# The low halves of the first MoE's third weight matrix: from one VectorE operation to two on Pool

## Chip, cores and metric

The kernel runs on one core of a Trainium2 chip. The metric is the device time of one execution in microseconds (us). Engines are named as the profile names them: PE is TensorE's matmul, PEld its weight load, DVE is VectorE, ACT is ScalarE, POOL is GpSimd, SP is SyncE, which issues the DMAs.

## What is computed

Causal attention with a forgetting bias over 4 batches, 8 heads, 576 positions and 64 columns per head; its output, seen as 2304 tokens of 512 columns, goes through two feed-forward blocks ("MoE" in the code), one after the other:

```python
rms = np.sqrt(np.mean(x * x, axis=-1, keepdims=True) + 1e-06)
xn = x / rms * rms_g
g = xn @ w_gate                       # 512 -> 1536
silu = g * (1.0 / (1.0 + np.exp(-g)))
val = xn @ w_val                      # 512 -> 1536
x = silu * val @ w_out                # 1536 -> 512: the matrix of this change
h = x @ w_in                          # second block, 512 -> 2048
return (h - np.tanh(h)) @ w_out2
```

The weights arrive as 64-bit floats, and the kernel decodes them itself.

## The kernel before

Every large product is made of three fp16 matmuls: each operand is split into a high half (the value rounded to fp16) and a low half (the rest). `mm3` issues high times high (line 693), high times the other's low half (694) and low times high (695).

The tokens are cut into six blocks of 384. `moe1_groups(j)` lists the work of block j: 24 up-projections, in turn `up1_g` (gate) and `up1_v` (value), of 12 matmuls each, and then four down-projections `down1` of 36 matmuls each. Between these groups the main loop steps the attention forward by a unit (a few heads of one query tile), so that the tokens of the next block are ready in time. A unit is: scores on PE (lines 452, 453), exponential on ACT (460), the causal mask on POOL (462), high half on ACT (467), low half on POOL (474), then products with v on PE (496 to 498). Its row maxima come earlier, from PE (409) and DVE (411).

Products of a group land in one of two PSUM buffers `mm`. The buffer of a gate group is read by ACT (710, tanh) and then DVE (711), that of a value group by DVE (720); ACT then makes the high half `sh` (721) and POOL the low half `sl` (722). The buffer of a down-projection is read by ACT (731). PE may write a buffer again only after its last reader.

The third matrix `w_out` is the tile `wo`, twelve pieces of 128 x 512, three for each of the four down-projections. While block 0 runs, each piece is loaded, decoded on DVE (559 to 561), squared on ACT (250); a sum over a group of three gives its scale `tau` (chain of small DVE operations, lines 666 to 669, and `iom` on POOL, 670); then `conv` splits the piece by `split`: ACT writes the high half (575), DVE the low half (576). Where these lie matters:

```python
    def slot_f(W, n):                       # the piece in fp32
        return W[:, n + 1, :].bitcast(FP32)
    def slot_h(W, n):
        return W[:, n, 0:512]
    def slot_l(W, n):
        return W[:, n, 512:1024]
```

The fp32 piece n - 1 fills exactly the place in which the two halves of piece n go. So the high half of piece n can be written only when the low half of piece n - 1 has been made: ACT, the engine of the low half, ACT, and so on, in series through all twelve pieces. Below, "slot n" is piece n counted from 0; slots 0 to 2 belong to the first down-projection.

The order of instructions on each engine is not written out by hand. A scheduler takes the program in the order of the code and sets the order by its own estimates of the costs; every engine then works through its queue strictly in that order. Loads of the next batch (q as `stv`, k as `stk`) run through SP's queue; ACT squares them on landing (line 250).

Of the kernel before, what the change touches and what calls it, by code (L numbers as in the profile page):

```python
# [11 lines left out]
ACTF = mybir.ActivationFunctionType  # L12
ALU = mybir.AluOpType
# [27 lines left out]
def tile_forget_attention_moe_moe2(ctx, tc, qa, qb, kt, va, vb, va0, vb0, s, wg, wv, wo, rg, win, wo2, out):  # L41
# [28 lines left out]
    V, A, G, P, SY = nc.vector, nc.scalar, nc.gpsimd, nc.tensor, nc.sync  # L70
# [17 lines left out]
    WO = w1.tile([128, 13, 1024], FP16, name="wo")  # L88
# [11 lines left out]
    def sm_tile(dtype=FP32):  # L100

        p, tag = (ps_mm, "mm") if early[0] else (ps_sm, "sm")
        return p.tile([128, 512], dtype, name=tag, tag=tag)
# [21 lines left out]
    def small(p, shape, dtype=FP32, tag=None):  # L125
        cnt[0] += 1
        return p.tile(shape, dtype, name=tag or f"sc{cnt[0]}", tag=tag or f"sc{cnt[0]}")

    def pow2inv(p, src, shape, emin, tag):
        e = small(p, shape, I32, tag + "e")  # L130
        V.tensor_scalar(out=e, in0=src.bitcast(I32), scalar1=24, scalar2=None, op0=ALU.logical_shift_right)
        V.tensor_scalar(out=e, in0=e, scalar1=float(emin), scalar2=50.0, op0=ALU.max, op1=ALU.add)
        V.tensor_scalar(out=e, in0=e, scalar1=23, scalar2=None, op0=ALU.logical_shift_left)
        sg = small(p, shape, FP32, tag + "s")
        V.reciprocal(out=sg, in_=e.bitcast(FP32))
        return e.bitcast(FP32), sg

    def ones_sum(psum, ss, n):
        P.matmul(out=psum[:, 0:n], lhsT=ones_f, rhs=ss, start=True, stop=True)
# [109 lines left out]
    def sq_accum(src, acc, junk=None):  # L249
        A.activation(out=src if junk is None else junk, in_=src, func=ACTF.Square, accum_out=acc)  # L250
# [300 lines left out]
    def decode(dst, src, raw):  # L551

        if src.dtype != I32:
            SY.dma_start(out=dst, in_=src)
            return
        with hold(1):
            SY.dma_start(out=raw, in_=src)
        d, hi, lo = dst.bitcast(I32), raw[:, :, 1], raw[:, :, 0]
        V.tensor_scalar(out=d, in0=hi, scalar1=3, scalar2=0x3FFFFFFF, op0=ALU.logical_shift_left, op1=ALU.bitwise_and)
        V.scalar_tensor_tensor(out=d, in0=hi, scalar=-0x40000000, in1=d, op0=ALU.bitwise_and, op1=ALU.bitwise_or)  # L560
        V.scalar_tensor_tensor(out=d, in0=lo, scalar=29, in1=d, op0=ALU.logical_shift_right, op1=ALU.bitwise_or)

    def slot_f(W, n):
# [9 lines that stand above are left out]
    def split(W, n, sc):  # L573
        src, hi, lo = slot_f(W, n), slot_h(W, n), slot_l(W, n)
        A.activation(out=hi, in_=src, func=ACTF.Copy, scale=sc)
        V.scalar_tensor_tensor(out=lo, in0=src, scalar=sc, in1=hi, op0=ALU.mult, op1=ALU.subtract)  # L576

    def raw_tile(p, bufs):
        return p.tile([128, 512, 2], I32, name="raw", tag="raw", bufs=bufs)

    def raw_slots(W, n):

        return W[:, n:n + 2, :].bitcast(I32).rearrange("p a (c w) -> p (a c) w", w=2)

    def junk16(raw):
        return raw[:, 0:128, :].bitcast(BF16).rearrange("p a b -> p (a b)")
# [50 lines left out]
    def wo_tasks(p):  # L637
        tasks = []
        tl = {}

        def first():
            sm3 = small(const, [128, 3], FP32, "sm3")
            for j in range(3):
                V.tensor_copy(sm3[:, j:j + 1], sig_s[j])
            smin = small(const, [128, 1], FP32, "smin")
            V.tensor_reduce(out=smin, in_=sm3, op=ALU.min, axis=AX.X)
            wos["ismin"] = small(const, [128, 1], FP32, "ismin")
            V.reciprocal(out=wos["ismin"], in_=smin)
            wos["rho"] = small(const, [128, 3], FP32, "rho")
            V.reciprocal(out=wos["rho"], in_=sm3)  # L650
            V.tensor_scalar(out=wos["rho"], in0=wos["rho"], scalar1=smin, scalar2=None, op0=ALU.mult)
            wos["iom"] = small(const, [128, 4], FP32, "iom")

        def piece(g, k):
            n = 3 * g + k
            raw = raw_slots(WO, 9 + 2 * (n // 2 % 2)) if n < 8 and n % 2 else raw_tile(p, 2)
            decode(slot_f(WO, n), wo[g, :, k], raw)
            if k == 0:
                wos["ss", g] = small(const, [128, 3], FP32, f"woss{g}")
            sq_accum(slot_f(WO, 3 * g + k), wos["ss", g][:, k:k + 1], junk16(raw))  # L660

        def chain(g):
            ps = sm_tile()
            ones_sum(ps, wos["ss", g], 3)
            nm = small(const, [128, 1], FP32, f"won{g}")
            V.tensor_reduce(out=nm, in_=ps[:, 0:3], op=ALU.add, axis=AX.X)
            isg, sg = pow2inv(const, nm, [128, 1], 37, f"wo{g}")
            tl["tau", g] = small(const, [128, 3], FP32, f"tau{g}")
            V.tensor_scalar(out=tl["tau", g], in0=wos["rho"], scalar1=sg, scalar2=None, op0=ALU.mult)
            G.tensor_scalar(out=wos["iom"][:, g:g + 1], in0=isg, scalar1=wos["ismin"], scalar2=1.0, op0=ALU.mult, op1=ALU.mult)  # L670

        def conv(g, k):
            split(WO, 3 * g + k, tl["tau", g][:, k:k + 1])

        tasks.append(first)
        for g in range(4):
            for k in range(3):
                tasks.append(lambda g=g, k=k: piece(g, k))
            tasks.append(lambda g=g: chain(g))
            for k in range(3):  # L680
                tasks.append(lambda g=g, k=k: conv(g, k))
        return tasks
# [243 lines left out]
    def need(T):  # L926
        return sum(len(units(x)) for x in range(T + 1)) + 2
# [26 lines left out]
    while last0 not in done_norm:  # L954
# [3 lines left out]
        n = min(left[0], 1)  # L958
# [5 lines left out]
    for j in range(NBLK - 1):  # L964
        last = BLOCK_TILES[j + 1][1] - 1
        s0 = steps[0]
        n = min(need(last), total) - s0
# [435 lines left out]
```

## Time and profile before

| | us |
|---|---|
| three runs, median (lowest to highest) | 1070.36 (1068.99 to 1070.47) |
| the profiled execution | 1068.06 |
| its span in the trace | 1066.3 |
| PE busy in the span | 973.4 (91%) |
| DVE busy | 679.9 (64%) |
| ACT busy | 606.6 (57%) |
| POOL busy | 320.6 (30%) |

The span is the time between the first and the last instruction; 1.8 us of the execution lie around it. A matmul of 384 columns shows about 0.33 us but follows its predecessor after 0.16 us, since matmuls are pipelined. What PE costs is therefore read from the distance of starts, and what it loses from its idle time, with the engine that ended it.

### The profile page before, as it was taken

Reading aid. Unit: us, or ns where it says so; the run is one execution under the profiler, and the core shown is the slowest. Engines: PE = TensorE matmul, PEld = TensorE weight load, DVE = VectorE, ACT = ScalarE, POOL = GpSimd, SP = SyncE. Lnnn points to the kernel's source line nnn. Section 1 sums busy time; section 2 is a strip of 40 time slices with the busy share of each in tenths; the row PEclk is TensorE's granted clock in tenths of the full one; section 3 lists DMA queues with packets and bytes.
Section 4 is the critical chain, followed back from the end, with each engine's and each line's share of the span. In section 5 each row is a group of like instructions: output and inputs, shape, how many; then the busy total and the mean of one; then the engine's idle time right before and its main releaser. Section 6 shows DMA issues by size and latency. Waiting matters only on the chain.

```text
span 1066.3 us, 19297 instructions
## 1 busy us (share of the span) xinstructions
PE 973.4 (91%) x7472; PEld 616.0 (58%) x7472; DVE 679.9 (64%) x1472; ACT 606.6 (57%) x1172; POOL 320.6 (30%) x405
## 2 busy tenths in 40 slices
PE   1488878799899999999999899999999999999998
PEld 1366545456566666666666555655666666666664
DVE  8987998975585641574553878579792683438500
ACT  6589657766675763676767456446571462225400
POOL 5121266323462542364456102100200251015200
PEclk9977988999999999999999999999999999999999
DMA  8614524231212112210200970142102000000000
GB/s 266 260 36 105 179 88 134 73 100 61 65 38 53 23 46 70 82 28 17 58 19 11 292 247 5 45 135 68 60 1 82 8 2 16 23 23 1 8 23 30
DMA packets 49438, 76.81 MB, mean 72 GB/s; under 512 B 25890, under 2 KB 35202, under 8 KB 48834
## 3 DMA queue, kind: packets, MB, share of 16 engines
q1 hardware_dynamic: 49346, 75.58, 23.0%
q8 instruction: 58, 0.95, 0.4%
q14 instruction: 34, 0.28, 0.1%
HBM read 59.42 MB, written 9.55 MB: 65 GB/s over the span
## 4 chain that ended last, share of the span: by engine, by line
PE 62%; DVE 18%; DMA 8%; ACT 5%; issue 4%; POOL 1%; SPq 1%; ACTq 0%; DVEq 0%; POOLq 0%
PE m L693 10%; PE m L695 10%; PE m L694 10%; PE mm L693 8%; PE mm L695 8%; PE mm L694 8%; DMA stv<-qb 1%; DVE w L560 1%; PE st L452 1%; PE st L453 1%; DMA raw<-wo 1%; DVE tm L711 1%; DMA w<-wo 1%; PE pv L494 1%; DVE r L417 1%
## 5 line engine op out<-in xcount | busy, mean ns | idle before, releaser
L693 PE MATMUL mm<-xth,w 128*128 128x384 f16 x480 | 161.3, 336 | 24.3 <-DVE tm L711 18.2
L694 PE MATMUL mm<-xtl,w 128*128 128x384 f16 x480 | 161.0, 336 | 0.9 <-DMA xtl<-xl 0.9
L695 PE MATMUL mm<-xth,w 128*128 128x384 f16 x480 | 160.4, 335 | 0.1
L694 PEld LDWEIGHTS <-w 128*128 128x128 f16 x960 | 94.8, 99 | 86.1 <-issue 32.4
L695 PEld LDWEIGHTS <-w 128*128 128x128 f16 x960 | 94.7, 99 | 64.8 <-issue 5.0
L693 PEld LDWEIGHTS <-w 128*128 128x128 f16 x960 | 95.3, 99 | 62.2 <-issue 4.0
L693 PE MATMUL m<-dh,w 128*128 128x384 f16 x384 | 124.1, 326 | 0.7 <-ACT t L1269 0.7
L694 PE MATMUL m<-dl,w 128*128 128x384 f16 x384 | 124.4, 326 | 0.0
L695 PE MATMUL m<-dh,w 128*128 128x384 f16 x384 | 124.1, 326 | 0.0
L722 POOL TENSOR_TENSOR sl<-tm,sh 128x384 f16<-128x384 f32 x72 | 76.2, 1059 | 112.9 <-ACT sh L721 103.7
L474 POOL TENSOR_TENSOR phl<-pf,phl 128x512 f16<-128x512 f32 (+2 forms) x90 | 97.4, 1090 | 40.6 <-ACT phl L467 39.1
L462 POOL TENSOR_SCALAR_AFFINE_SELECT pf<-pf 128x128 f32<-128x128 f32 (+3 forms) x105 | 43.1, 413 | 175.9 <-ACT pf L460 172.4
L1261 POOL TENSOR_SCALAR io<-iso,isd 128x1 f32<-128x1 f32 x24 | 12.0, 501 | 257.1 <-ACT t L1269 257.1
L460 ACT ACTIVATE pf<-st,lnp,ilam 128x512 f32<-128x512 f32 (+2 forms) x105 | 73.0, 703 | 24.7 <-PE st L453 19.3
L1269 ACT ACTIVATE t<-m,io 128x384 f32<-128x384 f32 x24 | 13.8, 578 | 126.7 <-PE m L695 123.0
L693 PE MATMUL mm<-sh,wo 128*128 128x384 f16 x240 | 78.0, 326 | 2.3 <-DVE tm L711 2.3
L695 PE MATMUL mm<-sh,wo 128*128 128x384 f16 x240 | 78.2, 326 | 0.7 <-DVE wo L576 0.7
L694 PE MATMUL mm<-sl,wo 128*128 128x384 f16 x240 | 78.1, 326 | 0.0
L452 PE MATMUL st<-q,kl 128*128 128x128 f16 (+1 forms) x456 | 62.5, 216 | 9.1 <-DVE q L368 2.7
L1300 DVE SCALAR_TENSOR_TENSOR c<-m,sigma,c 128x768 f32<-128x768 f32 x32 | 32.5, 1015 | 57.3 <-PE m L695 55.6
L1289 POOL TENSOR_TENSOR dl<-c,dh 128x768 f16<-128x768 f32 x28 | 48.0, 1730 | 54.9 <-ACT dh L1288 54.9
L711 DVE SCALAR_TENSOR_TENSOR tm<-tm,mm 128x384 f32<-128x384 f32 x60 | 32.9, 548 | 43.9 <-ACT tm L710 41.4
(369 smaller groups left out, 2571.0 us busy)
## 6 DMA issues: line engine op xcount, KB each, us to landing
raw<-wo SPq DMA_DIRECT2D x16, 512.0 KB
w<-win SPq DMA_DIRECT2D x16, 512.0 KB
wo<-wg SPq DMA_DIRECT2D x12, 512.0 KB
wo<-wv SPq DMA_DIRECT2D x12, 512.0 KB
stk<-kt SPq DMA_DIRECT2D x4, 1152.0 KB
x2d<-tm SPq DMA_DIRECT2D x24, 192.0 KB
x2f<-x2d SPq DMA_DIRECT2D x6, 768.0 KB
out<-t SPq DMA_DIRECT2D x24, 192.0 KB
```

Of the source, the lines that this page charges most:

```text
L452: P.matmul(out=ps[:, o:o + w], lhsT=K2[sl][:, ks], rhs=q2_of(T)[:, h, 0:w], start=True, stop=False)
L460: A.activation(out=pf[:, 0:o], in_=ps[:, 0:o], func=ACTF.Exp, scale=bstate[b]["ilam"][:, hh:hh + 1], bias=lnp)
L462: G.affine_select(out=dg, in_=dg, pattern=[[0, len(heads)], [1, w]], compare_op=ALU.is_ge, fill=0.0, base=0, channel_multiplier=-1)
L474: G.tensor_tensor(out=u["pl"][:, 0:n], in0=u["pf"][:, 0:n], in1=u["ph"][:, 0:n], op=ALU.subtract)
L693: P.matmul(out=ps, lhsT=wh, rhs=xh, start=first, stop=False)
L694: P.matmul(out=ps, lhsT=wh, rhs=xl, start=False, stop=False)
L695: P.matmul(out=ps, lhsT=wl, rhs=xh, start=False, stop=last)
L711: V.scalar_tensor_tensor(out=t, in0=t, scalar=1.0, in1=ps, op0=ALU.add, op1=ALU.mult)
L722: moe_pend.append(lambda: G.tensor_tensor(out=SH["l"][:, f, :], in0=t, in1=SH["h"][:, f, :], op=ALU.subtract))
L1269: A.activation(out=t, in_=ps, func=ACTF.Copy, scale=io)
L1289: by.tensor_tensor(out=DL[:, s8, ds, :], in0=c[:, ds], in1=DH[:, s8, ds, :], op=ALU.subtract)
L1300: V.scalar_tensor_tensor(out=out, in0=ps, scalar=sg, in1=c0, op0=ALU.mult, op1=ALU.add)
```

## The change

Only `conv` of the third matrix changes. ACT makes the high half as before. POOL then multiplies the fp32 piece by its scale in place, and subtracts the high half from it in a second operation, whose result is the low half. DVE has no part in it any more. `split` itself, which the other matrices use, stays.

```diff
         def conv(g, k):
-            split(WO, 3 * g + k, tl["tau", g][:, k:k + 1])
+            n, sc = 3 * g + k, tl["tau", g][:, k:k + 1]
+            A.activation(out=slot_h(WO, n), in_=slot_f(WO, n), func=ACTF.Copy, scale=sc)
+            G.tensor_scalar(out=slot_f(WO, n), in0=slot_f(WO, n), scalar1=sc, scalar2=1.0, op0=ALU.mult, op1=ALU.mult)
+            G.tensor_tensor(out=slot_l(WO, n), in0=slot_f(WO, n), in1=slot_h(WO, n), op=ALU.subtract)
```

The scaling in place overwrites what ACT reads, so it waits for ACT; the subtraction waits for the scaling.

The scheduler also sets another order around it. Twelve DVE instructions are gone and 24 are added on POOL. On PE the two orders are the same up to row 2167 of 14520 and again from row 3995 on (weight loads counted); DVE, ACT, POOL and SP have such a stretch too, in the same part of the program: the down-projections of block 0 and the whole of block 1. In the changed kernel the line numbers behind the edit are higher by three.

On DVE, at the end of block 0's up-projections, before (line 711 reads the PSUM buffer that the first down-projection needs):

```order
L720 SCALAR_TENSOR_TENSOR tm<-tm,mm 128x384
L576 SCALAR_TENSOR_TENSOR wo<-wo,tau_2416 128x512
L561 SCALAR_TENSOR_TENSOR wo<-raw,wo 128x512
L544 SCALAR_TENSOR_TENSOR ss<-ss 128x1
L132 TENSOR_SCALAR wo1e<-wo1e 128x1
L131 TENSOR_SCALAR wo2e<-won_2528 128x1
L514 RECIPROCAL rr<-rr 128x4
L559 TENSOR_SCALAR wo<-raw 128x512
L711 SCALAR_TENSOR_TENSOR tm<-tm,mm 128x384
```

The same place on DVE after the change (711 is now line 714, 720 line 723):

```order
L132 TENSOR_SCALAR wo1e<-wo1e 128x1
L131 TENSOR_SCALAR wo2e<-won_2534 128x1
L514 RECIPROCAL rr<-rr 128x4
L559 TENSOR_SCALAR wo<-raw 128x512
L543 TENSOR_SCALAR ss<-ss 128x1
L133 TENSOR_SCALAR wo1e<-wo1e 128x1
L132 TENSOR_SCALAR wo2e<-wo2e 128x1
L560 SCALAR_TENSOR_TENSOR wo<-raw,wo 128x512
L544 SCALAR_TENSOR_TENSOR ss<-ss 128x1
L135 RECIPROCAL wo1s<-wo1e 128x1
L133 TENSOR_SCALAR wo2e<-wo2e 128x1
L714 SCALAR_TENSOR_TENSOR tm<-tm,mm 128x384
```

Lines 723, 561 and 544 stand directly ahead of this piece. The split is gone from between 723 and 561, and the next piece's decode (560) with six small operations now stands ahead of 714.

On ACT, the high halves around slot 3 before (575 is the high half, `stv` the two halves of q of the next batch, squared by line 250):

```order
L575 ACTIVATE wo<-wo,tau_2467 128x512
L516 ACTIVATE x<-pv,rr 128x64 x4
L575 ACTIVATE wo<-wo,tau_2467 128x512
L516 ACTIVATE x<-pv,rr 128x64 x4
L250 ACTIVATE stv,ssqk<-stv 128x1152
L250 ACTIVATE xl,ss<-x 128x512
L575 ACTIVATE wo<-wo,tau_2467 128x512
L731 ACTIVATE tm<-mm,iom 128x384
L250 ACTIVATE stv,ssqk<-stv 128x1152
```

The same place after (the high half is line 674; tau_2416 is the scale of slots 0 to 2, tau_2470 that of 3 to 5):

```order
L516 ACTIVATE x<-pv,rr 128x64 x8
L674 ACTIVATE wo<-wo,tau_2416 128x512
L250 ACTIVATE xl,ss<-x 128x512
L250 ACTIVATE stv,ssqk<-stv 128x1152 x2
L674 ACTIVATE wo<-wo,tau_2470 128x512
L545 ACTIVATE xh<-x,ss 128x512
L734 ACTIVATE tm<-mm,iom 128x384
L433 ACTIVATE rt<-sm 16x128
L674 ACTIVATE wo<-wo,tau_2470 128x512
L460 ACTIVATE pf<-st,lnp,ilam 128x384 x2
```

Both squares of `stv` now stand ahead of the high half of slot 3, where two of that group's high halves stood ahead of the first of them. Further down, the square of `stk` stands ahead of the high half of slot 6; before, it stood behind all twelve.

On POOL, from the end of block 0's up-projections, before:

```order
L722 TENSOR_TENSOR sl<-tm,sh 128x384
L670 TENSOR_SCALAR iom<-wo1e,ismin 128x1
L670 TENSOR_SCALAR iom<-wo2e,ismin 128x1
L722 TENSOR_TENSOR sl<-tm,sh 128x384
L670 TENSOR_SCALAR iom<-wo3e,ismin 128x1
L462 AFFINE_SELECT pf<-pf 128x128 x2
L474 TENSOR_TENSOR phl<-pf,phl 128x384 x2
```

After, from the last `sl` (now line 725) of block 0 on:

```order
L725 TENSOR_TENSOR sl<-tm,sh 128x384
L676 TENSOR_TENSOR wo<-wo 128x512
L675 TENSOR_SCALAR wo<-wo,tau_2416 128x512
L670 TENSOR_SCALAR iom<-wo3e,ismin 128x1
L676 TENSOR_TENSOR wo<-wo 128x512
L675 TENSOR_SCALAR wo<-wo,tau_2470 128x512
L676 TENSOR_TENSOR wo<-wo 128x512
L675 TENSOR_SCALAR wo<-wo,tau_2470 128x512
L676 TENSOR_TENSOR wo<-wo 128x512
L462 AFFINE_SELECT pf<-pf 128x128 x2
L675 TENSOR_SCALAR wo<-wo,tau_2470 128x512
L474 TENSOR_TENSOR phl<-pf,phl 128x384
```

The subtractions of slots 1 and 2 stand behind the last `sl` and behind `iom` of group 3, and from slot 5 on masks and low halves of the attention stand between the two operations of a slot. On PE the 144 matmuls of the four down-projections, which ran nearly together, are now cut into some 18 pieces with scores and products of the attention between them, while the up-projections of block 1 have more even fillings.

## Rows read from the trace of the kernel before

**Rows 1.** Page, part 1: busy time, share of the span, instructions.

```profile
PE 973.4 (91%) x7472; PEld 616.0 (58%) x7472; DVE 679.9 (64%) x1472; ACT 606.6 (57%) x1172; POOL 320.6 (30%) x405
```

**Rows 2.** Windows: stretch, length, busy time by engine, clock, DMA.

```profile
217.00:345.00 128.00, 119.81 (x1001) 76.58 (x998) 83.73 (x202) 84.79 (x173) 48.92 (x64) 0.99 0.23 64
217.00:265.00 48.00, 46.50 (x362) 28.75 (x359) 29.96 (x91) 32.40 (x63) 12.20 (x18) 1.00 0.29 85
265.00:275.00 10.00, 6.91 (x50) 3.98 (x48) 9.27 (x16) 6.96 (x15) 4.26 (x5) 0.83 0.19 49
```

**Rows 3.** Waits of PE, 217 to 345: total us, times, longest.

```profile
PE mm L693 <- DVE tm L711: 6.5, 6, 2.5
...
PE mm L695 <- DVE wo L576: 0.7, 2, 0.4
```

**Rows 4.** Timeline of PE: start, duration, line, operation, [idle before and its releaser].

```profile
218.35 0.32 PE L693 MATMUL mm<-sh,wo 128*128 128x384 f16 x1 [0.84 <-DVE tm L711]
...
263.60 0.33 PE L694 MATMUL mm<-xtl,w 128*128 128x384 f16 x1
263.76 0.33 PE L695 MATMUL mm<-xth,w 128*128 128x384 f16 x1
...
267.77 0.48 PE L693 MATMUL mm<-xth,w 128*128 128x384 f16 x1 [2.53 <-DVE tm L711]
...
270.87 0.33 PE L694 MATMUL mm<-xtl,w 128*128 128x384 f16 x1
```

**Rows 5.** Timeline of ACT and DVE: high and low halves in series.

```profile
231.00 0.75 DVE L576 SCALAR_TENSOR_TENSOR wo<-wo,tau 128x512 f16<-128x512 f32 x1
...
231.79 0.72 ACT L575 ACTIVATE wo<-wo,tau 128x512 f16<-128x512 f32 x1 [0.82 <-DVE wo L576]
...
232.54 0.75 DVE L576 SCALAR_TENSOR_TENSOR wo<-wo,tau 128x512 f16<-128x512 f32 x1 [0.22 <-ACT wo L575]
```

**Rows 6.** Groups by form, POOL: count, busy us, mean ns of one, idle.

```profile
L474 POOL TENSOR_TENSOR phl<-pf,phl 128x384 f16<-128x384 f32 x24 | 22.2, 931 | 11.1 <-ACT phl L467 10.6
L462 POOL TENSOR_SCALAR_AFFINE_SELECT pf<-pf 128x128 f32<-128x128 f32 x56 | 18.7, 334 | 114.9 <-ACT pf L460 111.7 <-PE mm L695 2.2 <-PE pv L498 0.8
```

**Rows 7.** Timeline of POOL; x2 and x4 are rows merged.

```profile
212.72 3.26 POOL L474 TENSOR_TENSOR phl<-pf,phl 128x512 f16<-128x512 f32 x2 [0.47 <-ACT phl L467]
...
221.19 1.50 POOL L722 TENSOR_TENSOR sl<-tm,sh 128x384 f16<-128x384 f32 x1 [0.77 <-ACT sh L721]
...
310.29 1.16 POOL L474 TENSOR_TENSOR phl<-pf,phl 128x512 f16<-128x512 f32 x1 [0.24 <-ACT phl L467]
...
312.52 2.69 POOL L318 TENSOR_SCALAR vt<-stv,vs 128x512 f16<-128x512 f32 x4 [0.20 <-DVE vs L135]
```

**Rows 8.** Timeline of DVE at the end of block 0's up-projections.

```profile
214.89 1.64 DVE L561 SCALAR_TENSOR_TENSOR wo<-raw,wo 128x512 int32<-128x512 int32 x1
...
217.76 0.54 DVE L711 SCALAR_TENSOR_TENSOR tm<-tm,mm 128x384 f32<-128x384 f32 x1
...
219.19 0.68 DVE L560 SCALAR_TENSOR_TENSOR wo<-raw,wo 128x512 int32<-128x512 int32 x1
...
220.45 0.68 DVE L561 SCALAR_TENSOR_TENSOR wo<-raw,wo 128x512 int32<-128x512 int32 x1
```

**Rows 9.** Timeline of ACT: squares of the loads, copies of k.

```profile
226.26 1.16 ACT L250 ACTIVATE stv<-stv 128x1152 f32<-128x1152 f32 x1 [0.59 <-DMA stv<-qb]
...
243.29 2.12 ACT L250 ACTIVATE kl<-stk 128x2304 bf16<-128x2304 f32 x1 [0.85 <-DMA stk<-kt]
...
262.06 2.77 ACT L289 ACTIVATE kc<-stk,qks 64x576 f16<-64x576 f32 x4 [1.50 <-DVE qks L259]
```

**Rows 10.** Timeline of SP: issues of the loads of q and k.

```profile
222.59 0.42 SPq L227 DMA_DIRECT2D stv<-qb  x1
...
225.12 0.43 SPq L227 DMA_DIRECT2D stv<-qb  x1
...
237.51 0.58 SPq L236 DMA_DIRECT2D stk<-kt  x1
```

## The prediction

> **What bounds the kernel now.** Three views, in this order. The page: PE is busy for 91% of the span [rows 1], so a gain has to be PE's idle time or its clock, and what DVE saves counts only where PE waited for DVE. The windows: PE's order is changed only from about 217 to 345 us (block 0's down-projections and block 1), and there it is busy for 119.8 of 128 us [rows 2]; 8.2 us are idle. The waits of PE in that stretch [rows 3]: 6.5 us in six waits are DVE's line 711, which frees a PSUM buffer, and only 0.7 us in two waits are the split that the change removes. The longest, 2.53 us, has a second price: the next ten matmuls take 267.77 to 270.87, 3.1 us, where ten at the usual distance of 0.16 take 1.6 [rows 4]; the granted clock of that stretch is 0.83 [rows 2], some 3 of its 10 us at 1.2 in place of 2.4 GHz. So 1.5 us more are lost. Of the 8.2 us, 0.84 end at 218.35, where the first down-projection starts [rows 4]. What can be won behind that point is 7.35 + 1.5 = 8.8 us.
>
> **What the change removes.** Twelve splits of 0.75 us [rows 5] make 9.0 us of DVE. They lie in a stretch where PE loses 1.5 of 48 us [rows 2]. Their own waits are worth 0.7; the rest would have to come through 711.
>
> **What it adds.** Two POOL operations for a slot. The subtraction has the form of line 474, which took 1.16 us alone and 1.63 (3.26 for two) while DVE worked on SBUF beside it [rows 7]. The scaling has the form of line 318, 2.69 / 4 = 0.67 us [rows 7], but writes fp32 where 318 writes fp16; no row shows that. I take 0.7, with ends of 0.67 and, by the same stretch of 1.63 / 1.16, 0.95. The Trainium skill (GPSIMD Engine Reference, section 3.1) gives a body bound by its ports 1.03 cycles an element: at its 1.2 GHz an estimate of 0.44 us for 512, against the 0.67 of the row; by it each slot below would be about 0.25 us shorter and the sum about 2 us lower.
>
> The sum of POOL's new work (12 x 1.86 = 22 us) decides nothing, since POOL is 30% busy [rows 1]. What decides is that the slots are in series: the high half of a slot waits for the low half of the slot ahead. Before, one round was 231.00 to 232.54, 1.54 us [rows 5]: 0.72 on ACT, 0.75 on DVE, some 0.04 for each handover. After, it is 0.72 + 0.70 + 1.16 and three handovers, **2.7 us**. From slot 3 to slot 11's first need of a low half, the new order gives PE 98 matmuls of down-projections (16.0 us), one group of an up-projection (2.0) and 54 scores, 63 products and 14 maxima, which by their widths I put at 8.2: 26.2 us for eight rounds, **3.3 a round**. So the bare chain is not the bound; it has 0.6 us to spare a round. But other things stand in it. I walk the new order with durations of the rows.
>
> (a) *Start.* Before, line 711 began at 217.76 [rows 8] and the first down-projection at 218.35. In the new order a split of 0.75 is no longer ahead of it, but line 560, 0.68 [rows 8], and six small operations are. The five operations between 561 and 711 took 217.76 - 216.53 = 1.2 us [rows 8], two of them larger, so I put the six at about 0.75, an estimate. 711 comes about 0.7 us later, and PE starts at 219.05: **0.7**.
>
> (b) *Slots 1 and 2.* POOL's subtraction for slot 1 stands behind the last `sl`, which began at 221.19 and took 1.50 [rows 7]. It ends at 222.6 now, about as before, and the low half is there at 223.75. PE has done slot 0 and its fillings by 222.3: **1.4**. Slot 2's stands behind `iom` of group 3, whose DVE chain has three maxima between its steps: low half at about 226.7, PE there 0.6 earlier: **0.6**.
>
> (c) *Slot 3.* A free chain would give 226.7 + 2.7 = 229.4. But ACT now has both squares of `stv` ahead of the high half. The first load landed at 226.2, 3.6 us after its second issue [rows 9, 10]; the second, issued at 225.12 [rows 10] and now about 0.5 earlier, lands near 228.2; its square takes 1.16 [rows 9] and the read of its sum a little more, the high half starts at 229.5 and the low half is there at 232.1. PE, which gets through the first two matmuls of the slot without the low half, stands from 228.7: **3.4**, and as that is longer than the 2.53 of rows 4, **1.5** for the clock.
>
> (d) *Slots 4 to 11.* Eight rounds of 2.7 are 21.6 us. Between the steps POOL now has seven masks and seven low halves of the attention, 7 x (0.33 + 0.93) = 8.8 us [rows 6], which stop the chain where they stand between scaling and subtraction. ACT has the copies of k, 2.77 [rows 9], and, ahead of slot 6, the square of `stk`: its load took from 237.51 to 243.2 [rows 9, 10]; in the new order SP issues it near 234.9, behind the second transposes, so the square ends near 242.9, 2.3 us after slot 5's low half. Item by item I get from 232.1 to about 265.4 for slot 11's low half, 33.3 us or 4.2 a round, against 26.2 of PE: **7.1**.
>
> (e) *Block 1.* The 8.8 us fall away, since the groups stand elsewhere. The chain of k, whose DVE step 291 held up 711 for the 2.53 us, runs beside down-projections now. But three times a 291 still stands directly ahead of a 711. I take **2.2**, with ends of 0.5 and 5.
>
> Sum: 0.7 + 1.4 + 0.6 + 4.9 + 7.1 + 2.2 - 8.8 = +8.1 us. Against the profiled execution that is 1068.06 + 8.1 = 1076.2; the median of the runs stands 2.3 us above it, so the forecast is **1078.5 us**. What comes behind 345 us has the same order on all engines and is shifted with PE.
>
> Ends: low, 0.7 + 1.0 + 0.3, slot 3 with the free chain (0.7, no clock loss), (d) at 0 and (e) at 0.5 give 3.2 - 8.8 = -5.6, 1064.8. High, scaling 0.95 and subtraction 1.63 add 0.72 for each of eight slots, 5.8, and (e) is 5, 2.8 more: +16.7, 1087.
>
> **Rivals.**
>
> *The chain keeps up, and DVE's relief is won: faster.* The second `stv` lands before its turn and POOL's attention work falls into gaps of the chain, so that a round stays under 3.3 us, PE's own pace. That is the point from which it decides: below it PE hardly waits for a low half. Then (d) is 1 and (c) 0.7: 0.7 + 1.4 + 0.6 + 0.7 + 1 + 0.5 - 8.8 = -3.9, 1066.5. For it: before, POOL was busy for 12.2 of the 48 us [rows 2], PE waited 0.7 us for splits in all [rows 3], and the bare chain has its 0.6 to spare. Against: every step of the chain stands in a queue behind loads and attention.
>
> *Even.* New stalls of the down-projections and old ones of block 1 balance: (c) costs 2 without a clock loss, (d) 3.6: 0.7 + 1.4 + 0.6 + 2 + 3.6 + 1 - 8.8 = +0.5, 1070.9. A chain of about 3.8 us a round does that.
>
> *POOL and DVE slow each other.* Line 561 took 1.64 us beside POOL's subtractions and 0.68 otherwise [rows 8]. With twelve pairs more on POOL this meets DVE's decode, 546 and 291, the last of these ahead of 711; with the slow POOL prices it is the high end, 1087. For it: every subtraction beside DVE in rows 7 is long. Against: once the decode is done, DVE has little on SBUF in the new order until block 1. The Trainium skill (GPSIMD Engine Reference, section 8) says that the engine shares its SBUF interfaces with VectorE and contends with instructions that have two SBUF inputs; the trace agrees, 1.64 against 0.68.
>
> **How the numbers follow.** Forecast (1073 to 1083) 0.55, faster rival (1064 to 1068) 0.20, even (1068 to 1073) 0.17, slow end (1083 to 1090) 0.08. A measurement of this kernel can tell some 0.2%, 2.1 us, from no change: 1068.2 to 1072.5 is "same". Faster 0.21 (its rival and an edge of the even case), same 0.17, slower 0.62. The range from 1066 to 1085 leaves out about half of the faster rival and most of the slow end, 0.17.
>
> **What would show it.** In the changed trace PE's waits between 219 and 266 us should name POOL's line 676, together 9 to 12 us, with one of over 2.5 us at slot 3 that ends with a low half whose high half waited for the square of `stv`, and a clock below 1.0 behind it. A round of the chain should be 2.7 us where nothing stands in it. The high half of slot 6 should start when the square of `stk` ends. In block 1 the waits for 714 (711 before) should shrink from 6.5 to about 2 us. The prediction is wrong if POOL's scaling takes over 1 us or under 0.5, if `stv` has landed before ACT gets to it, or if PE's waits for low halves stay below 5 us in all.

## The result, and the profile after

The changed kernel takes 1081.28 us (median of 4 runs, 1080.24 to 1082.38), the kernel before 1069.67 beside it. The ratio is 1.0111, with a 95% interval of 1.0094 to 1.0128: slower by 11.6 us. The forecast was 1078.5, the range 1066 to 1085. The profiled execution took 1081.83 us with a span of 1080.1.

In the code after, what follows line 676 stands three lines lower: VectorE's 711 is 714, TensorE's 693 to 695 are 696 to 698, and 722 is 725. The two operations on Pool are 675 (scale, in place) and 676 (subtraction), the high half is 674.

The page, part 1, of the changed kernel answers to [rows 1]:

```profile
PE 978.9 (91%) x7471; PEld 619.0 (57%) x7472; DVE 668.0 (62%) x1460; ACT 608.0 (56%) x1172; POOL 344.0 (32%) x429
```

VectorE's work fell by 12 us and Pool's rose by 23, and neither number tells the result. The windows of the changed kernel do (the columns of [rows 2]; the first two stretches answer to it):

```profile
217.00:345.00 128.00, 111.08 (x913) 69.45 (x909) 71.20 (x187) 84.29 (x169) 70.05 (x87) 0.97 0.22 61
217.00:265.00 48.00, 36.03 (x291) 21.05 (x287) 24.74 (x81) 32.44 (x63) 30.91 (x40) 0.96 0.31 88
...
230.00:235.00 5.00, 3.09 (x12) 1.35 (x11) 0.75 (x1) 1.66 (x4) 3.87 (x4) 0.73 0.37 93
...
270.00:275.00 5.00, 3.08 (x20) 1.63 (x18) 1.88 (x3) 4.90 (x10) 1.94 (x3) 0.82 0.23 84
275.00:280.00 5.00, 5.00 (x40) 3.20 (x38) 2.37 (x7) 4.08 (x12) 4.08 (x4) 0.84 0.07 15
```

From 217 to 265 us TensorE is busy for 36.0 of 48 us, where it was busy for 46.5. The granted clock falls to 1.2 GHz twice, for 3.4 us each time, once in the window from 230 us and once in the one from 270; before it fell once, in the window from 265. The waits of TensorE in that stretch (total us, times, longest) answer to [rows 3]:

```profile
PE mm L696 <- DVE tm L714: 4.4, 3, 2.2
PE mm L698 <- POOL wo L676: 4.1, 5, 1.9
PE pv L496 <- ACT phl L467: 1.7, 1, 1.7
PE mm L696 <- ACT wo L674: 1.4, 2, 1.1
PE sm L431 <- DVE r L428: 1.1, 2, 0.9
PE sm L409 <- DVE r L411: 0.9, 3, 0.4
PE sm L409 <- ACT qc L365: 0.7, 1, 0.7
```

Only 5.5 us name a half of the weight (4.1 a low half of Pool's, 1.4 a high half of ACT's). The rest names operands of the attention (`phl`, `r`, `qc`) and VectorE's 714. Both kernels can be compared at one landmark, a transpose of line 431 behind the changed stretch (the kernel before above, the changed one below):

```profile
354.89 0.22 PE L431 MATMUL sm<-ident,r 128*16 128x128 f16 x1
...
367.83 0.22 PE L431 MATMUL sm<-ident,r 128*16 128x128 f16 x1
```

It stands 12.9 us later. (The two profiled executions lie 13.8 us apart, the medians 11.6.) The first down-projection starts 1.1 us later, and behind that start, up to the landmark, TensorE is idle for 14.0 us where it was for 8.5 (sums of its idle rows, each of over 0.15 us). What the slow clock takes (one minus the granted clock, summed over windows of 5 us) is 3.4 us where it was 1.7. That makes 1.1 + 5.5 + 1.7 = 8.3. The other 4.6 stand in no idle row, but most of them can be read from the distances of starts, each set against the usual distance of its kind of matmul. At an interruption the last matmul runs out its 0.33 us where its successor would have followed after 0.16: the 21 idle rows lose 17.4 us of distance with 14.0 of idle time, the 10 before 10.1 with 8.5, which is 1.7 us more. Eleven interruptions of under 0.15 us (before one) lose 2.5 us where it was 0.2, which is 2.3 more.

### The profile page after: what moved, and what is told of

Same layout as the page of the kernel before. It is cut to its first block, busy times and chain, and to the rows that moved or that the text cites. A ratio compares the mean times of both kernels' runs of the same rounds, so it can differ in the third digit from the quotient of the medians.

```text
span 1080.1 us, 19305 instructions
## 1 busy us (share of the span) xinstructions
PE 978.9 (91%) x7471; PEld 619.0 (57%) x7472; DVE 668.0 (62%) x1460; ACT 608.0 (56%) x1172; POOL 344.0 (32%) x429
## 4 chain that ended last, share of the span: by engine, by line
PE 64%; DVE 17%; DMA 8%; ACT 5%; issue 4%; POOL 2%; SPq 1%; another core or an unknown queue 0%; ACTq 0%; DVEq 0%; POOLq 0%
PE m L696 11%; PE m L697 11%; PE m L698 11%; PE mm L696 8%; PE mm L698 8%; PE mm L697 8%; DMA wo<-wv 2%; DVE w L560 1%; PE st L452 1%; PE st L453 1%; DMA raw<-wo 1%; PE pv L494 1%; DVE w L559 1%; DVE q L368 1%; DVE r L417 1%
## 5 line engine op out<-in xcount | busy, mean ns | idle before, releaser
L725 POOL TENSOR_TENSOR sl<-tm,sh 128x384 f16<-128x384 f32 x72 | 73.7, 1024 | 111.5 <-ACT sh L724 104.3
L1272 ACT ACTIVATE t<-m,io 128x384 f32<-128x384 f32 x24 | 13.8, 578 | 126.7 <-PE m L698 123.0
```

The lines of the kernel that those rows point to most:

```text
L725: moe_pend.append(lambda: G.tensor_tensor(out=SH["l"][:, f, :], in0=t, in1=SH["h"][:, f, :], op=ALU.subtract))
L1272: A.activation(out=t, in_=ps, func=ACTF.Copy, scale=io)
```

## The experiments

Two reasons were to be told apart. **T**, the prediction's: high half on ACT, scale and subtraction on Pool and the next high half stand in series, and TensorE waits for that chain. **R2**: the scheduler has laid out this stretch anew around the longer operations, and that layout costs the time, with or without Pool. **R1** was the prediction's slow rival: Pool and VectorE slow each other. In each run the kernel before ran beside; ratios are to it. Numbers of lines differ from kernel to kernel; the names of the tiles tell which line is which. Costs in us are differences of medians.

### TensorE's order alone held

To part the operation from the layout, a kernel is first laid out by the scheduler with one form of the lower halves; the order of TensorE's instructions is kept (`want`), and the kernel with the other form is built with edges that force this order (`traced` are its instructions):

```diff
+                for a, b in zip(seq, seq[1:]):
+                    tc.add_manual_dep(traced[e][b], traced[e][a].name, mybir.DependencyInfo(mybir.DependencyClass.NoSync, mybir.DependencyReason.DATA), reason="order")
...
-    nc, _ = build("pool")
+    _, want = build("dve")
+    nc, _ = build("pool", want)
```

> The pair of Pool operations as in the changed kernel, but TensorE's instructions forced into the order that they have in the kernel before (edges of order on TensorE alone; the other engines' order is free). Theory T (the chain of high half on ACT, scale and subtraction on Pool, next high half, a bare round of 2.7 us, is what TensorE waits for): the loss stays, 1077 to 1086 us, with TensorE waiting 9 us or more for the halves of `wo` or for DVE's L714 behind them. Rival R2 (the loss is the re-arranged order of TensorE's work, not Pool's price): back to 1068 to 1072 us. Rival R1 (Pool and VectorE slow each other): as T, 1077 to 1084, but with Pool's subtractions at 1.5 us or more each.

Measured: 1083.82 us, ratio 1.0146 (1.0120 to 1.0173), in the ranges of T and of R1; the subtractions of 1.5 us or more that R1 asks for did not come, their mean is 1.26.

> VectorE's single operation for the lower halves as before, but TensorE's instructions forced into the order that they have in the changed kernel. T: 1068 to 1073 us, since the round of the chain is then about 1.7 us, half of what TensorE takes for a slot. R2: 1079 to 1083 us, since the order is the changed kernel's. R1: 1068 to 1072 us, since Pool's pair is gone.

Measured: 1082.86 us, 1.0130 (1.0108 to 1.0152), in the range of R2.

With the changed kernel's order on TensorE two more kernels were built, one in which nothing waits for Pool's pair and one in which the chain is cut. In both the conversions are queued behind all loads of the weight, and in the first `t` and `u` are scratch memory:

```diff
+                split(WO, n, sc)
...
+                G.tensor_scalar(out=t, in0=t, scalar1=sc, scalar2=1.0, op0=ALU.mult, op1=ALU.mult)
+                G.tensor_tensor(out=u, in0=t, in1=slot_h(WO, n), op=ALU.subtract)
```

> As the run with VectorE's single operation in the changed kernel's order, and beside it Pool carries out the same pair of operations for each slot on scratch memory, behind the same high half, with nothing waiting for the results (their outputs are not used; two memsets on VectorE are added). Pool's load and its meeting with VectorE stay, the chain is gone. T: within 2 us of that run, 1068 to 1075 us. R1: 1077 to 1084 us, nearly all of the changed kernel's loss. R2: like that run.

Measured: 1090.01 us, 1.0201 (1.0175 to 1.0227), above every range.

```diff
+                t = slot_f(WO, n) if n < 3 else raw_tile(p, 2)[:, 0:256, :].rearrange("p a b -> p (a b)").bitcast(FP32)
+                G.tensor_scalar(out=t, in0=slot_f(WO, n), scalar1=sc, scalar2=1.0, op0=ALU.mult, op1=ALU.mult)
+                G.tensor_tensor(out=slot_l(WO, n), in0=t, in1=slot_h(WO, n), op=ALU.subtract)
```

> The changed kernel with TensorE's order kept, but from the fourth slot on Pool writes the scaled piece to a scratch buffer in place of the piece itself, so that the next high half waits for the scale alone, and the scale no longer waits for the high half. The same Pool work, the chain cut. T: the waits of slots 3 to 11 (7.6 + 3.05 us and 1.6 us of slow clock in the changed kernel) mostly go, what remains is the start, slots 1 and 2 and block 1: 1070 to 1074 us. R1 and R2: 1079 to 1082 us, since Pool does as much and the order is the same.

Measured: 1092.12 us, 1.0216 (1.0196 to 1.0235), above every range too. TensorE's waits of this last kernel, 217 to 345 us:

```profile
PE st L456 <- DMA qc<-rt: 4.9, 2, 4.5
PE sm L412 <- ACT qc L368: 2.7, 1, 2.7
PE pv L501 <- POOL phl L477: 2.3, 1, 2.3
PE mm L708 <- POOL wo L681: 2.3, 3, 1.0
```

Three of the four missed what T expects, and they settle little. The waits for halves did go (2.3 us are left, of the slots that still scale in place), but others of up to 4.5 us came for the attention's operands. The reason may lie in the setup: with TensorE's order fixed from outside and the other engines free, the traces have ACT in another order than the kernel whose order was held at 33 to 55 places, and in the first two kernels VectorE at 43 and 30, so these kernels compare more than one thing. They suggest that the order weighs as much as the operation, and that it has to be held on all engines.

### The orders of all engines held

The same edges on all five engines; only the lower halves themselves, on VectorE or Pool, are free. The diff is as the first above, with the loop over all engines in place of TensorE. In the run with the split the conversions are queued behind all loads; its trace has the changed kernel's order on TensorE, VectorE, ACT and SyncE all the same.

> VectorE's single operation as before, and every other instruction of all five engines in the order that it has in the changed kernel (only the place of the lower halves themselves is free). Theory T (Pool's price in the chain is what TensorE waits for, whatever the order): with the chain's round back at about 1.7 us the time comes back to 1068 to 1073 us. Rival R2 (the scheduler laid the work out around a slower chain, and that layout by itself costs the time): 1078 to 1083 us, with waits of TensorE for the scores' and softmax's operands in place of those for `wo`.

Measured: 1080.44 us, 1.0097 (1.0080 to 1.0115). So **the changed kernel's layout costs 10 us with VectorE's single operation and without Pool's pair**. TensorE's waits from 217 to 345 us, and below them the timeline of ACT before slot 3 and of TensorE at slots 3 and 6 (start, duration, line, [idle before and its releaser]):

```profile
PE mm L709 <- ACT wo L579: 3.9, 2, 2.1
PE sm L413 <- DVE r L415: 2.4, 3, 1.2
PE mm L709 <- DVE tm L727: 2.4, 4, 1.7
PE sm L413 <- ACT qc L369: 1.8, 1, 1.8
PE pv L500 <- ACT phl L471: 1.7, 1, 1.7
```

```profile
226.55 1.16 ACT L254 ACTIVATE stv<-stv 128x1152 f32<-128x1152 f32 x1 [0.81 <-DMA stv<-qb]
...
227.71 0.71 ACT L579 ACTIVATE wo<-wo,tau 128x512 f16<-128x512 f32 x1
...
228.48 0.50 PE L709 MATMUL mm<-sh,wo 128*128 128x384 f16 x1 [2.10 <-ACT wo L579]
...
241.72 0.34 PE L709 MATMUL mm<-sh,wo 128*128 128x384 f16 x1 [1.84 <-ACT wo L579]
```

No wait names a low half. TensorE is idle for 14.4 us behind the start of the first down-projection, up to the landmark, where it is 14.0 in the changed kernel. It stalls at the same places: at slot 3, where ACT squares the second load of the queries ahead of the high half (1.14 + 1.91 us in the changed kernel, 2.10 here), at slot 6 behind the square of the keys (0.29 + 0.96 there, 1.84 here), at the maxima and at `phl` (1.70 in both).

> Pool's pair, and every other instruction of all five engines in the order of the kernel before. T: 1078 to 1086 us, TensorE waits 8 us or more for the halves of `wo`, and no instruction but the lower halves has another place. R2: 1068 to 1072 us. Both causes (the pair costs some 10 us in the old order, and the new order costs as much with or without it): this one as T, and the run with the split in the new orders as R2.

Measured: 1077.72 us, 1.0083 (1.0056 to 1.0111). So **the pair costs 7.6 us where nothing else is moved** (6 to 12 by the interval of the ratio). TensorE's waits (217 to 345 us), one of them in its timeline, and a round on ACT and Pool:

```profile
PE mm L710 <- POOL wo L688: 7.2, 10, 1.1
PE mm L708 <- DVE tm L726: 5.7, 6, 2.7
```

```profile
234.13 0.72 ACT L686 ACTIVATE wo<-wo,tau 128x512 f16<-128x512 f32 x1 [0.44 <-POOL wo L688]
...
234.95 0.69 POOL L687 TENSOR_SCALAR wo<-wo,tau 128x512 f32<-128x512 f32 x1 [0.85 <-ACT wo L686]
235.73 1.15 POOL L688 TENSOR_TENSOR wo<-wo 128x512 f16<-128x512 f32 x1
...
236.91 0.72 ACT L686 ACTIVATE wo<-wo,tau 128x512 f16<-128x512 f32 x1 [2.06 <-POOL wo L688]
...
236.94 0.34 PE L710 MATMUL mm<-sh,wo 128*128 128x384 f16 x1 [0.49 <-POOL wo L688]
```

Here the chain is seen bare: a round from high half to high half is 236.91 - 234.13 = 2.78 us, and TensorE is released when the subtraction ends. Its waits for low halves were two of 0.7 us in all [rows 3]; now they are ten of 7.2. The waits for VectorE's 711 (726 here) fell from 6.5 to 5.7 only.

The two costs, 7.6 and 10.4 us, do not add up to the changed kernel's 11.6. In the new layout the pair adds only about 1 us to what the layout costs without it, and the intervals of the two ratios overlap, so that this 1 us isn't told from nothing.

### The high halves ahead of the squares

ACT's order of the changed kernel (`seq`, of which `hi` are the twelve high halves), with two high halves moved; all other orders as in the changed kernel (here too the conversions are queued behind all loads):

```diff
+    for k in (hi[3], hi[6]):
+        p = seq.index(k)
+        while "Square" in t[seq[p - 1]] and ("stv" in t[seq[p - 1]] or "stk" in t[seq[p - 1]]):
+            p -= 1
+        seq.remove(k)
+        seq.insert(p, k)
```

> The changed kernel in its own orders on all engines, but on ACT the high half of slot 3 goes ahead of the two squares of the queries' loads (1.16 us each), and that of slot 6 ahead of the square of the keys' load (2.11 us). T, by the prediction's steps (c) and (d): slot 3's high half starts near 226.8 us in place of 229.0, TensorE's two waits there (1.14 and 1.91 us) shrink by about 2 us and the 1.6 us of slow clock behind them go, slot 6's half by 1 us: 1076 to 1079 us, 2 to 5 us less than the changed kernel. If the squares are not what holds the halves, or if another operand is late next: 1080 to 1082 us.

Measured: 1081.81 us, 1.0112 (1.0088 to 1.0135), the changed kernel's time. The timeline of TensorE:

```profile
228.55 0.34 PE L709 MATMUL mm<-sh,wo 128*128 128x384 f16 x1 [0.42 <-POOL wo L686]
...
231.06 0.34 PE L707 MATMUL mm<-sh,wo 128*128 128x384 f16 x1 [0.70 <-ACT wo L684]
...
233.59 0.22 PE L457 MATMUL st<-qc,kc 128*128 128x128 f16 x1 [2.04 <-DMA qc<-rt]
...
242.59 0.22 PE L456 MATMUL st<-q,kl 128*128 128x128 f16 x1 [1.17 <-ACT pf L464]
...
247.84 0.39 PE L413 MATMUL sm<-kc,qc 128*128 128x512 f16 x1 [1.83 <-ACT qc L369]
```

The waits at slots 3 and 4 shrank as expected (1.14 + 1.91 became 0.42 + 0.70), but TensorE came to scores whose query rows were still on their way (at 231.55 us, where the changed kernel starts them at 235.81 without a wait), and stood there for 2.04; further on it stood for `pf` and `qc`, 1.17 and 1.83 us (0.25 and 0.72 in the changed kernel). What is saved on the halves is given back at the next operand that is late. So the squares are one of several things that are late in this layout, and moving them alone gives nothing back.

### The chain itself, in the old layout

Three kernels in the orders of the kernel before, on all engines, to try T where nothing else moves; the edits are shown against `conv` of the changed kernel. A third operation:

```diff
             G.tensor_scalar(out=slot_f(WO, n), in0=slot_f(WO, n), scalar1=sc, scalar2=1.0, op0=ALU.mult, op1=ALU.mult)
+            G.tensor_scalar(out=slot_f(WO, n), in0=slot_f(WO, n), scalar1=1.0, scalar2=1.0, op0=ALU.mult, op1=ALU.mult)
             G.tensor_tensor(out=slot_l(WO, n), in0=slot_f(WO, n), in1=slot_h(WO, n), op=ALU.subtract)
```

> Pool's pair in the old orders of all engines, with a third operation between scale and subtraction (the piece scaled once more, by 1.0, in place; 0.69 us). In the run with the pair in the old orders a slot took 3.0 us from 225.31 to 249.33 us, of which TensorE waited 0.76 us. Theory T (the serial chain sets the pace there): each of some 10 rounds grows by 0.7 to 0.8 us and all of it is TensorE's wait, 7 to 8 us on top of that run: 1083 to 1088 us. If something else holds TensorE there: 1077 to 1080 us.

Measured: 1085.12 us, 1.0152 (1.0129 to 1.0175): 7.4 us above the run with two operations. TensorE's wait, 217 to 345 us:

```profile
PE mm L716 <- POOL wo L690: 14.3, 10, 1.8
```

Ten waits of 7.2 us became ten of 14.3, which is 0.71 a round for an operation of 0.62 and its handover.

The same pair on VectorE:

```diff
-            G.tensor_scalar(out=slot_f(WO, n), in0=slot_f(WO, n), scalar1=sc, scalar2=1.0, op0=ALU.mult, op1=ALU.mult)
-            G.tensor_tensor(out=slot_l(WO, n), in0=slot_f(WO, n), in1=slot_h(WO, n), op=ALU.subtract)
+            V.tensor_scalar(out=slot_f(WO, n), in0=slot_f(WO, n), scalar1=sc, scalar2=1.0, op0=ALU.mult, op1=ALU.mult)
+            V.tensor_tensor(out=slot_l(WO, n), in0=slot_f(WO, n), in1=slot_h(WO, n), op=ALU.subtract)
```

> The same two operations, scale in place and subtraction, but both on VectorE, in the old orders of all engines. T: a round is ACT 0.72, scale 0.4, subtraction 0.7 and the gaps, about 2.1 us, under TensorE's own 2.25 us a slot: 1069 to 1073 us. If the form with two operations in place is what costs, on whichever engine: 1076 to 1080 us.

Measured: 1072.74 us, 1.0034 (1.0021 to 1.0048). TensorE's waits for low halves, and the two operations (count, shortest/median/longest ns, first and last start):

```profile
PE mm L715 <- DVE wo L689: 2.4, 3, 1.3
```

```profile
L688 DVE TENSOR_SCALAR wo<-wo,tau x12: 460/486/532, 215.1 to 246.0; 128x512 f32<-128x512 f32 x12
L689 DVE TENSOR_TENSOR wo<-wo x12: 678/691/693, 217.4 to 246.6; 128x512 f16<-128x512 f32 x12
```

The form in two operations costs 2.5 us here; Pool's price makes it 7.6.

The scaled piece beside the chain, in a slot of W1's tile that is free by then:

```diff
-            G.tensor_scalar(out=slot_f(WO, n), in0=slot_f(WO, n), scalar1=sc, scalar2=1.0, op0=ALU.mult, op1=ALU.mult)
-            G.tensor_tensor(out=slot_l(WO, n), in0=slot_f(WO, n), in1=slot_h(WO, n), op=ALU.subtract)
+            t = slot_f(W1, 23)
+            G.tensor_scalar(out=t, in0=slot_f(WO, n), scalar1=sc, scalar2=1.0, op0=ALU.mult, op1=ALU.mult)
+            G.tensor_tensor(out=slot_l(WO, n), in0=t, in1=slot_h(WO, n), op=ALU.subtract)
```

> Pool's pair for all twelve slots in the old orders of all engines, with the scaled piece written to a slot of the first weights' tile that is free by then (the one behind the last piece of W1) and not in place. As much work on Pool as in the changed kernel, but the next high half waits for the scale alone and the scale for no high half. T: Pool needs 1.85 us a slot against TensorE's 2.25: 1068 to 1073 us. R1 (Pool's work beside VectorE's costs by itself): 1076 to 1082 us.

Measured: 1071.50 us, 1.0013 (0.9999 to 1.0026). TensorE's wait for low halves, and Pool's two operations:

```profile
PE mm L716 <- POOL wo L690: 1.7, 2, 1.4
```

```profile
L689 POOL TENSOR_SCALAR w<-wo,tau x12: 681/694/1234, 210.8 to 241.5; 128x512 f32<-128x512 f32 x12
...
L690 POOL TENSOR_TENSOR wo<-w,wo x12: 1156/1159/1695, 212.1 to 242.6; 128x512 f16<-128x512 f32 x12
```

The same work on Pool, at the same prices, and no loss that can be told from none. So in the old layout nearly all of the 7.6 us is the series, and R1 falls as the cause: Pool's work beside VectorE's costs 1.2 us, at most 2.8 by the interval. It does slow VectorE: line 368 (372 here) at 240.4 us takes 1.57 us here and took 0.74 at 240.5 before, when Pool stood idle; yet the kernel's time shows little of it. The run also shows that the edges by themselves cost nothing that can be told from none.

### Other layouts

Is any fresh layout as bad? Two kernels were left to the scheduler. In both the twelve conversions are queued behind all loads and norms of the weight:

```diff
             tasks.append(lambda g=g: chain(g))
+        for g in range(4):
             for k in range(3):
                 tasks.append(lambda g=g, k=k: conv(g, k))
```

The first keeps VectorE's split.

> The kernel before, with VectorE's single operation, where the twelve conversions are merely queued behind all the loads and norms of this weight and not between those of each group; the scheduler is free and lays out some 1,100 of TensorE's instructions in another order. R2 in its wide form (the old layout is a good one, and any fresh layout of this stretch costs): 1075 to 1082 us. In its narrow form (only the layout made for the slower chain costs): 1068 to 1072 us.

Measured: 1071.83 us, 1.0016 (1.0004 to 1.0029). The second has Pool's pair with the scaled piece in scratch for all slots.

> The pair on Pool for all twelve slots with the scaled piece in a scratch buffer and not in place, the scheduler free to order all (the conversions are queued behind all loads of the weight, for the buffers). T: the chain's round is ACT's 0.70 us and Pool's 0.69 us with no wait between them, Pool's own rate 1.85 us a slot against TensorE's 3.3: 1068 to 1074 us. R2 (any re-arranged order costs about 10 us): 1078 to 1085 us.

Measured: 1078.54 us, 1.0088 (1.0067 to 1.0110). Its waits of TensorE, 217 to 345 us:

```profile
PE mm L698 <- DVE tm L716: 4.1, 4, 1.6
PE sm L415 <- DVE r L417: 2.4, 1, 2.4
PE mm L698 <- ACT tm L736: 2.0, 1, 2.0
PE sm L139 <- ACT raw L250: 1.8, 1, 1.8
```

A fresh layout need not cost: in the trace of the first, 692 of TensorE's 7,472 places hold a matmul of another kind than in the kernel before (821 in the changed kernel, 783 in the second), and it lost 1.5 us. The second lost 8.5 with no wait for a low half; its waits are for PSUM buffers, for operands of the attention and for a norm. They are not the whole of it: in its profiled execution, the longest of its six, the slow clock takes 10.2 us up to the landmark, where it took 1.7 before. With the chain cut as well, the old layout had lost 1.2. So what a layout costs is a matter of the layout, not of how many rows it moves. Why the scheduler's layouts around Pool's pair are worse was not tried further, nor which of the moved rows would have to go back.

## Why the prediction was right, and where it was not

The time and its sign were right (1081.3 against 1078.5), and the likeliest case came. The reason was half right, and part of the agreement is luck.

**What bounds it.** Right: what VectorE was spared is worth little. In the old layout, with Pool's pair, the waits for 711 fell by 0.8 of 6.5 us.

**The chain.** Right as a mechanism, with its sizes: the scale took 0.69 us (predicted 0.70) and the subtraction 1.15 (1.16), and the bare round, in the run with the pair in the old orders, 2.78 (2.7). The groups of the changed kernel (ns, shortest/median/longest):

```profile
L675 POOL TENSOR_SCALAR wo<-wo,tau x12: 691/692/1213, 212.2 to 265.9; 128x512 f32<-128x512 f32 x12
L676 POOL TENSOR_TENSOR wo<-wo x12: 1152/1154/1677, 214.4 to 266.7; 128x512 f16<-128x512 f32 x12
```

By the estimate from the Trainium skill (GPSIMD Engine Reference, section 3.1), 0.44 us, the scale would be a third shorter than here; the measurement decides, as the row of line 318 had. The same section gives some 2.6 cycles an element for two inputs, an estimate of 1.11 us for the subtraction; the measured 1.15 agrees.

**(a)** 0.7 predicted, 1.1 measured: the first down-projection starts at 219.47. The decode ahead of 714 ran beside Pool's rows of this stretch, 559 for 1.25 us and 560 for 1.09, where they took 0.39 and 0.68 before. **(b)** 2.0 predicted, 1.1 measured (0.20, 0.26 and 0.61). **(c)** 3.4 and 1.5 of clock predicted; 1.14 + 1.91 = 3.05 and 1.7 measured, in two waits and not in one of over 2.5. The rows of ACT and of TensorE at slot 3 and slot 6 answer to [rows 4, 9]:

```profile
219.47 0.32 PE L696 MATMUL mm<-sh,wo 128*128 128x384 f16 x1 [2.19 <-DVE tm L714]
...
227.84 1.16 ACT L250 ACTIVATE stv<-stv 128x1152 f32<-128x1152 f32 x1 [0.31 <-DMA stv<-qb]
...
229.00 0.70 ACT L674 ACTIVATE wo<-wo,tau 128x512 f16<-128x512 f32 x1
...
232.17 0.45 PE L698 MATMUL mm<-sh,wo 128*128 128x384 f16 x1 [1.91 <-POOL wo L676]
...
240.40 2.11 ACT L250 ACTIVATE kl<-stk 128x2304 bf16<-128x2304 f32 x1
...
242.50 0.71 ACT L674 ACTIVATE wo<-wo,tau 128x512 f16<-128x512 f32 x1
```

The second load landed at 227.8 (predicted 228.2) and the low half was there at 232.17 (232.1); slot 6's high half starts as the square of `stk` ends. **(e)** 2.2 predicted, 2.2 measured for 714. The layout does this, not VectorE's relief: with the split on VectorE in the same orders these waits are 0.6 us.

**(d), the step that failed.** 7.1 us of waits for low halves were predicted for slots 4 to 11. TensorE is idle for 5.6 there, but only 1.7 of it names a half; 4.0 names `phl`, `pf`, `qc`, `r` and the query rows. The prediction wanted 9 to 12 us of waits that name 676 and said it would be wrong below 5: they are 4.1. From slot 3's low half to slot 11's the chain took even longer than predicted, 35.7 us (33.3), so that it was not the price of a round that was wrong, but that TensorE would stand for the halves. The prediction walked the new order with one clock, the chain, and took the attention's rows between the slots for filling that is always ready. They have chains of their own on ACT and VectorE, and in this layout these are as late as the halves. The run with the split in the new orders fits this: the chain's round is short there, and it loses nearly as much. Step (c) had the layout in its hands (the squares ahead of the high half come from ACT's new order, and stall TensorE for 2.10 us without any Pool), and booked it to the chain.

**What was left out.** The sum was +8.1 us on the profiled execution, and the landmark moved by 12.9. Not in the sum were the wait of 1.70 us for `phl` and 0.23 behind it at 272, the second fall of the clock that follows it (1.7 us), and the 4.0 us that more interruptions cost beside their idle rows (1.7 and 2.3 above); against them (b) and (d) were 2.4 us too large. That the median came within 2.8 us is luck: from one profiled execution to the other the time moved by 13.8 us where 8.1 were forecast, and the 2.3 us that the forecast adds for the median hid about half of the difference.

**The rivals.** *Pool and VectorE slow each other*: single operations of Pool do stretch (0.69 to 1.21 us beside line 561, 1.15 to 1.68 beside 291 and 368), and VectorE's too, as in (a). The Trainium skill (GPSIMD Engine Reference, section 8) says that Pool contends with VectorE's instructions that have two SBUF inputs; 561 and 368 are such, so the trace agrees. But the medians are the quiet prices, and the cut chain shows that in the old layout the whole work is nearly free. *The chain keeps up*: it would need a round below TensorE's own pace. In the old layout that pace, without waits, was (24.0 - 6.1) / 8 = 2.25 us a slot from 225.31 to 249.33, under the 2.78 of the round. In the new one rows of the attention stretch it: by the distances of starts, TensorE's work from 232.17 to 267.91 us is 24.8 us, 3.1 a slot (predicted 3.3). A bare round would have kept up with that, but these rows stood in the chain's queues and brought their own waits.

## What to carry to other kernels

When a buffer is reused in place along a series, price a new operation by what it adds to one round of the series, not by its engine's load: here 0.7 us in each of ten rounds was 7 us, and one free slot of scratch took nearly all of it away where the order was held. Where a scheduler sets the order, a change of one operation is two changes. Here they were told apart only with the order of every engine held; holding one engine alone mixed them again. In a new order, ask of each row that is moved between the steps of a chain whether its own operands are there, since it can be the next thing that is late.

## What the runs showed of the hardware

Of twelve in-place scales on Pool most took 0.69 us for 128x512 in fp32 and single ones up to 1.21; on VectorE the same operation took 0.49 and the subtraction 0.69 against Pool's 1.15. Beside Pool's added work VectorE's maxima, which read the products in PSUM, kept their length: the eight of line 411 with 128x512 between 212 and 272 us took 0.69 us each before and 0.66 to 0.69 after. Operations on SBUF did not: with the chain cut in the old layout, line 368 took 1.57 us beside Pool where it had taken 0.74. In the changed kernel TensorE's clock fell to its lower level behind waits of 1.1 and 1.9 us around 230 us and behind 1.7 and 0.2 us at 272, and each fall cost about 1.7 us; behind a wait of 1.9 us at 293 it did not fall.
